# Spreading attention more evenly over the projections, and turning the last two heads on the tensor engine

## The chip, the cores and the metric

One core of one Trainium2 chip runs the program. The metric is the device time of that core in microseconds (us), taken over several executions; the median is quoted with the lowest and highest run. Ratios are computed as the mean time of one kernel's runs over the mean of the other's of the same rounds, so they are not quite the ratio of the medians that are quoted beside them. A difference counts as faster or slower from 2% on.

## The reference

Two blocks follow each other: a recurrent memory attention over 64 segments of 32 tokens with 32 heads, and a mixer with an MLP. Cut to what matters here:

```python
def _A_ref(x, mem0, Wq, Wk, Wv, Wo, seg_len):
    mem = mem0                                  # 8 rows
    for s in range(n_seg):                      # 64 segments, one after the other
        h = concatenate([mem, x[segment s]])
        q, k, v = h @ Wq, h @ Wk, h @ Wv        # 32 heads of 128
        o = softmax(mask(q k^T * scale)) @ v
        o = o @ Wo
        mem = o[:, :M]                          # feeds the next segment
        outs.append(o[:, M:])
x = x + ga * _A_ref(layernorm(x) * (1 + ca) + sa, ...)
x = x + gb * _B_ref(...)                        # cut
```

## The kernel before

It guesses all memory rows first (from averaged segments), runs the attention of all segments at once with the guess (`Mold`), and then compares the memory rows that come out (`Macc`) with the guess. If they do not agree, a flag is set and a second, slow path runs until they do.

```python
TAU2 = 2.0 ** -14
def check_a(kt):                       # per block of the model dimension
    df = Macc - Mold                   # [cut to formulas]
    Mold[kt] = df * df - TAU2 * Macc * Macc
def check_b():
    pn = sum of Mold over the dimension          # one number per memory row
    okr = pn <= 0
    rmx = (min(okr) < 0.5)                       # memory comparison failed
    nb  = (softmax sums, weights or scales out of range)
    nc.vector.tensor_tensor(flag_s[:], rmx[:], nb[:], ALU.max)
    nc.scalar.dma_start(flag_d[:], flag_s[:])
...
first_pass(...)
with tc.If(cond > 0):
    ...
    with tc.For_i(0, MAX_EXTRA):                 # 64 times
        c2 = load_flag()
        tc.strict_bb_all_engine_barrier()
        with tc.If(c2 > 0):
            general_pass()                       # the slow path; sets the flag anew
```

The projections go by pairs of heads (`P_units`), each in three parts `s`: Q and K of the even head, V of both heads, Q and K of the odd head. Attention (`scores`, `outs`) of the pair before is woven between them. V is projected transposed (`VT`) and turned by a DMA (`to_v`) into one of two buffers, `Vs[h % 2]`; `outs` reads it:

```python
units += d[:6] + [lambda: to_v(2 * hp)] + d[6:] if s == 2 else d     # in P_units

def to_v(h):
    assert h < 2 or ("outs", h - 2) in state      # the old V has been used up
    nc.sync.dma_start_transpose(Vs[h % 2][:, :, 0:DH], VTs[h % 2][:]...)

def outs(h, j):                                   # j-th group of three tiles of segments
    V, O = Vs[h % 2], Os[h % 2]
    ... nc.tensor.matmul(ps[:rows, i, :], lhsT=E..., rhs=V[:k, t, 0:DH + 1])
    if j == 7:
        state["outs", h] = True

def flip(h):                                      # O to OT, by DMA
    nc.sync.dma_start_transpose(OT, O[0:96]);  nc.sync.dma_start_transpose(MT, O[96:112])
def keep(h):                                      # memory rows to OTm, OT to DRAM
    ... nc.gpsimd.dma_start(OTx_d[:, h // 8, :, h % 8, :]..., flat...)
```

The order in which the Python emits these units is the program order. The framework derives the semaphores from it: a reader waits for the last writer emitted before it.

The attention list is cut into pairs (`per_hp`), a waiting list is served first in, first out, and after the last projection the last pair runs among the first matmuls of the output projection `Wo` (`W_units`, operands `wstream` and `OTc`).

## Time and profile before

| | before |
|---|---|
| time | 1516.28 us median (1514.69 to 1516.72, 4 runs) |
| PE busy | 1429 of 1517 us (94%) |
| PE waits from 770 to 1000 us | 25.1 us |

In the profile PE is the tensor engine (TensorE) at matmuls and PEld the same engine loading weights; DVE is VectorE, ACT ScalarE, POOL GpSimd, and SP is SyncE, whose queue here only issues DMAs. The granted clock is the share of TensorE's full clock that the hardware let through; the DMA share is how busy the core's 16 DMA engines were. The page of the kernel before says how busy each engine was; the columns are busy us, share of the span and instructions:

```profile
span 1517.1 us, 24283 instructions
PE 1429.2 (94%) x9074; PEld 760.1 (50%) x9074; DVE 921.4 (61%) x1961; ACT 668.2 (44%) x1403; POOL 356.1 (23%) x490
```

PE is the bound, so time can come only from PE's idle time, from its work or from its clock. The waits of PE between 770 and 1000 us of the kernel before (who waited for whom; us in total, times, longest):

```profile
PE ps_o L713 <- DMA V<-VT: 13.6, 1, 13.6
PE acc L845 <- DMA wstream<-in_A_Wo_dram: 7.2, 1, 7.2
PE acc L845 <- DMA OTc<-OTx_d: 3.6, 2, 1.8
PE acc L845 <- DVE x L847: 0.4, 1, 0.4
PE acc L845 <- issue: 0.3, 1, 0.3
```

Why V of the last head is late is read from the timeline of the SP queue of the kernel before (start, us, queue, line, operation):

```profile
785.21 16.14 SPq L728 DMA_TRANSPOSE OT<-O  x1
801.45 1.54 SPq L729 DMA_TRANSPOSE MT<-O  x1
803.08 0.53 SPq L537 DMA_DIRECT2D wo<-in_A_Wo_dram  x1
803.66 5.33 SPq L650 DMA_TRANSPOSE V<-VT  x1
```

The transpose `OT<-O` holds the queue for 16.1 us, since its operand is not ready, and V stands behind it. PE's timeline of the kernel before then shows the wait and what follows it (start, us, engine, line, operation, operands; in square brackets the idle time just before, and what ended it):

```profile
800.20 1.89 PE L845 MATMUL acc<-wstream,OTc 128*128 128x512 bf16 x8
815.64 0.86 PE L713 MATMUL ps_o<-V,E 104*104 104x129 bf16 x6 [13.56 <-DMA V<-VT]
816.30 1.91 PE L845 MATMUL acc<-wstream,OTc 128*128 128x512 bf16 x4
```

Before the wait eight matmuls take 1.89 us, after it four take 1.91 us: half speed. The Trainium skill ("TensorE: Matmul & The Clock Gate", "What's actually happening") says that the PE clock halves after an idle window of about 3.4 us; this trace agrees, at a wait of 13.6 us.

### The profile page before, as it was taken

Reading aid. Unit: us, or ns where it says so; the run is one execution under the profiler, and the core shown is the slowest. Engines: PE = TensorE matmul, PEld = TensorE weight load, DVE = VectorE, ACT = ScalarE, POOL = GpSimd, SP = SyncE. Lnnn points to the kernel's source line nnn. Section 1 sums busy time; section 2 is a strip of 40 time slices with the busy share of each in tenths; the row PEclk is TensorE's granted clock in tenths of the full one; section 3 lists DMA queues with packets and bytes.
Section 4 is the critical chain, followed back from the end, with each engine's and each line's share of the span. In section 5 each row is a group of like instructions: output and inputs, shape, how many; then the busy total and the mean of one; then the engine's idle time right before and its main releaser. Section 6 shows DMA issues by size and latency. Waiting matters only on the chain.

```text
span 1517.1 us, 24283 instructions
## 1 busy us (share of the span) xinstructions
PE 1429.2 (94%) x9074; PEld 760.1 (50%) x9074; DVE 921.4 (61%) x1961; ACT 668.2 (44%) x1403; POOL 356.1 (23%) x490
## 2 busy tenths in 40 slices
PE   5699999999999999999996799999997999999998
PEld 3365555556555655555653344444443444444443
DVE  5827777677676676766751343363287657675684
ACT  2715666665656665665650020122533661046400
POOL 7501100000000000000010222122011654535625
PEclk9999999999999999999998999999999999999999
DMA  9577779877778876778689999994299784377812
GB/s 307 193 279 158 154 163 197 169 161 158 152 163 197 169 171 153 154 159 193 131 220 292 323 328 327 290 270 146 64 276 270 231 265 157 100 246 240 281 52 77
DMA packets 406900, 304.81 MB, mean 201 GB/s; under 512 B 203370, under 2 KB 359018, under 8 KB 404850
## 3 DMA queue, kind: packets, MB, share of 16 engines
q1 hardware_dynamic: 367920, 239.39, 61.3%
q0 software_dynamic: 9616, 33.05, 7.3%
q10 hardware_dynamic: 29234, 30.71, 6.6%
q8 instruction: 73, 1.20, 0.3%
q14 instruction: 57, 0.47, 0.1%
HBM read 200.82 MB, written 50.63 MB: 166 GB/s over the span
## 4 chain that ended last, share of the span: by engine, by line
PE 73%; DMA 8%; issue 6%; DVE 5%; ACT 4%; POOL 3%; SPq 1%; ACTq 0%; DVEq 0%; POOLq 0%
PE acc L607 28%; PE bank_b L1202 6%; PE acc L845 6%; PE bank_b L1151 6%; PE acc L995 4%; PE acc L328 4%; PE bank_d L1151 3%; PE bank_d L1202 2%; PE bank_e L1202 2%; PE ps_o L713 2%; PE ps_s L698 2%; PE acc L318 2%; PE acc L1078 2%; PE bank_e L1151 1%; DVE ln_st L104 1%
## 5 line engine op out<-in xcount | busy, mean ns | idle before, releaser
L845 PE MATMUL acc<-wstream,OTc 128*128 128x512 bf16 x960 | 214.7, 385 | 11.3 <-DMA wstream<-in_A_Wo_dram 7.2
L607 PEld LDWEIGHTS <-T 128*128 128x128 f16 x1408 | 131.1, 97 | 123.2 <-issue 7.4
L575 ACT COPY snap<-acc 128x480 f32<-128x480 f32 x264 | 146.6, 564 | 101.9 <-PE acc L607 91.3
L607 PE MATMUL acc<-hs,T 128*128 128x480 f16 x704 | 158.5, 365 | 4.9 <-ACT snap L575 3.8
L607 PE MATMUL acc<-hh,T 128*128 128x480 bf16 (+1 forms) x704 | 162.3, 366 | 0.5 <-DVE VT L579 0.5
L845 PEld LDWEIGHTS <-OTc 128*128 128x128 bf16 x960 | 94.4, 99 | 124.8 <-DMA wstream<-in_A_Wo_dram 7.4
L740 POOL DMA_DIRECT2D OTx_d<-OT x32 | 24.8, 775 | 511.4 <-DMA OT<-O 495.2
L1151 PEld LDWEIGHTS <-ring 128*128 128x128 f16 (+1 forms) x784 | 77.5, 99 | 109.5 <-issue 17.6
L702 ACT ACTIVATE E<-ps_s 99x495 bf16<-99x495 f32 (+2 forms) x160 | 86.3, 543 | 65.0 <-PE ps_s L698 63.3
L607 PE MATMUL acc<-hh,wq 128*128 128x480 bf16 x464 | 105.3, 366 | 0.0
L579 DVE TENSOR_TENSOR KT<-acc,snap 128x480 bf16<-128x480 f32 x116 | 74.6, 655 | 47.0 <-PE acc L607 45.4
L720 DVE TENSOR_TENSOR O<-ps_o,rin_all 99x384 bf16<-99x384 f32 (+1 forms) x192 | 96.6, 510 | 3.8
L713 PE MATMUL ps_o<-V,E 99*99 99x129 bf16 (+2 forms) x704 | 81.1, 222 | 16.0 <-DMA V<-VT 15.0
L713 PEld LDWEIGHTS <-E 99*99 99x99 bf16 (+2 forms) x704 | 69.2, 127 | 53.2 <-issue 20.4
L1202 PEld LDWEIGHTS <-hq 128*128 128x128 bf16 (+1 forms) x560 | 54.9, 98 | 66.0
L1116 ACT COPY snap<-bank_b 128x512 f32<-128x512 f32 x72 | 40.6, 583 | 102.0 <-PE bank_b L1202 58.3
L715 DVE RECIPROCAL rin_all<-ps_o 99x3 f32<-99x3 f32 (+2 forms) x256 | 43.3, 173 | 68.8 <-PE ps_o L713 67.9
L718 ACT ACTIVATE O<-ps_o,rin_all 99x128 bf16<-99x128 f32 x192 | 56.6, 368 | 61.8 <-DVE rin_all L715 61.7
L1021 DVE TENSOR_TENSOR ring<-ring 128x1024 f16<-128x1024 bf16 (+1 forms) x64 | 75.5, 1200 | 5.5 <-PE bank_b L1202 5.1
L704 DVE TENSOR_TENSOR E<-E,maskB 99x495 bf16<-99x495 bf16 (+1 forms) x128 | 47.3, 377 | 51.5 <-ACT E L702 51.2
L110 POOL TENSOR_TENSOR ln_rstd<-ln_ve,mhalf 128x1 f32<-128x1 f32 x64 | 35.2, 550 | 173.7 <-DVE ln_ve L108 129.8
L938 ACT ACTIVATE u<-x,ln_nmr,ln_rstd 128x1024 bf16<-128x1024 f32 x16 | 19.7, 1232 | 123.9 <-DVE ln_nmr L937 75.0
(223 smaller groups left out, 2569.9 us busy)
## 6 DMA issues: line engine op xcount, KB each, us to landing
wstream<-in_A_Wo_dram SPq DMA_DIRECT2D x29, 1024.0 KB, 9.0
OTx_d<-OT POOLq DMA_DIRECT2D x32, 512.0 KB, 7.5
wstream<-in_B_w_dram SPq DMA_DIRECT2D x28, 512.0 KB, 4.4
ring<-in_B_w_dram SPq DMA_DIRECT2D x28, 512.0 KB, 5.5
ring<-in_B_w_dram SPq DMA_DIRECT2D x8, 1792.0 KB, 10.0
OTc<-OTx_d SPq DMA_DIRECT2D x13, 1024.0 KB, 8.3
wq<-in_A_Wq_dram SPq DMA_DIRECT2D x16, 512.0 KB, 7.6
wk<-in_A_Wk_dram SPq DMA_DIRECT2D x16, 512.0 KB, 8.5
```

What stands on the lines that cost most here:

```text
L328: nc.tensor.matmul(acc[:, 0:CONV], lhsT=W[:, kt, hl * P:(hl + 1) * P], rhs=hh[:, kt, MAIN:MAIN + CONV], start=(kt == 0), stop=(kt == KT - 1))
L575: nc.scalar.copy(t[:], st[q][bank][:, 0:CH])
L579: nc.vector.tensor_tensor(view(d, i), chunks(st[q][bank]), chunks(st[q][s_]), ALU.add)
L607: nc.tensor.matmul(acc[:, 0:CH], lhsT=B[:, k, :], rhs=A[:, k, :], start=(j in (1, 2, 5) and k == 0), stop=(k == 3), skip_group_check=True)
L702: nc.scalar.activation(E[:rows, 0:o], ps[:rows, 0:o], ACT.Exp, scale=DH ** -0.5)
L713: nc.tensor.matmul(ps[:rows, i, :], lhsT=state["e", h, t // 5][:k, col0(t) - col0(t // 5 * 5):col0(t) - col0(t // 5 * 5) + rows], rhs=V[:k ...
L720: nc.vector.tensor_tensor(O[:rows, ts[0]:ts[0] + n, :], ps[:rows, 0:n, 0:DH], rin[:, :, None].to_broadcast([rows, n, DH]), ALU.mult)
L845: nc.tensor.matmul(accs[tt][:], lhsT=ot[hl // 4][:, hl % 4, tt * P:(tt + 1) * P], rhs=woc[hl // 4][:, hl % 4, :], start=(h == 0), stop=(h ...
L995: nc.tensor.matmul(acc[:], lhsT=w1s[:, kt, ct * P:(ct + 1) * P], rhs=zT[:, kt, b * 512:(b + 1) * 512], start=(kt == 0), stop=(kt == KT - 1))
L1021: return nc.vector.tensor_tensor(dst, a, b, op)
L1151: nc.tensor.matmul(acc[:], lhsT=B[:, k, q * P:(q + 1) * P], rhs=A[:, k, :], start=(start and k == 0), stop=(k == 3), skip_group_check=True)
L1202: nc.tensor.matmul(acc[:], lhsT=L3[:, k, i * P:(i + 1) * P], rhs=R3[:, k, :], start=(start and k == 0), stop=(k == 13), skip_group_check=True)
```

## The change

The intent is to fill that hole: attention gets further ahead of the end of the projections, the outputs `O` of the last two heads need no DMA transpose (their few memory rows still do) and no way through DRAM, and loads that are not urgent leave the crowded stretch. The diff, cut to its core:

```diff
-                    units += d[:6] + [lambda: to_v(2 * hp)] + d[6:] if s == 2 else d
+                    units += d[:3] + [lambda: to_v(2 * hp)] + d[3:] if s == 2 else d
@@ turns of the last two heads
+        def turn(h, c):                     # eight tiles of O at a time
+            pt = psS.tile([P, 8, P], BF16, name="ps_s")
+            for i, t in enumerate(ts):
+                nc.tensor.transpose(pt[:, i, 0:96], O[0:96, t, :], ident[0:96, 0:96])
+            ... copy to OT by ScalarE or VectorE; c == 2 also turns MT by DMA
@@ attention(): one list instead of one per pair
+                            if h >= H - 2:
+                                if j in (3, 6):
+                                    waiting.append((5 * h + g, lambda h=h, j=j: turn(h, j // 3 - 1)))
+                                elif j == 7:
+                                    waiting.append((5 * h + g + 1, lambda h=h, j=j: turn(h, 2)))
+                                    waiting.append((5 * h + g + 1, lambda h=h: keep(h)))
+                    waiting.sort(key=lambda w: w[0])
@@ pacing
+        done, ahead = 0, len(att) - int(len(att) * 1.45 / H)
-            interleave(att[hp], fill)
+            for i, u in enumerate(fill):
+                u()
+                upto = int(ahead * (hp + (i + 1) / len(fill)) / (NHP - 1))
+                for a in att[done:upto]:
+                    a()
+                done = upto
@@ tail
+        load_ot(3)                          # six heads from DRAM ...
+        for h in range(H - 2, H):           # ... and two from SBUF
+            nc.vector.tensor_copy(ots[3][1][:, h % 8 - 4, :], last_ot[h][:]...)
+                ld = nc.sync.dma_start(w1s[:], ...)
+                tc.add_manual_dep(ld.ins, marks[1].ins.name, ..., reason="Wo loads first")
+                nc.gpsimd.dma_start(gb_b[:], ...)          # was loaded in the tail
```

The list has 499 units with the turns in it, so `ahead` is 477.

## The prediction

> **What bounds the kernel now.** PE: the page has it busy 1429 of 1517 us (94%). Between 125 and 775 us (attention interleaved with projections) the windows view leaves it about 11 us idle. The hole is the end of attention, 783 to 880: PE's waits view has 13.6 us for `V<-VT`, 7.2 for `wstream<-in_A_Wo`, 1.8 + 1.8 for `OTc<-OTx_d`, 0.3 issue: 24.7 us. After the two long waits the timeline shows 128x512 matmuls at about 427 ns instead of 216; I estimate 5 to 6 us lost. The Trainium skill ("TensorE: Matmul & The Clock Gate", "What's actually happening") says the PE clock halves after an idle window of about 3.4 us; the trace agrees (granted clock 0.73 in 800-825, 0.88 in 850-875). About 30 us can be had.
>
> The V wait is a queue effect: in SP's timeline the last head's `V<-VT` goes out at 803.7, behind an `OT<-O` that held the queue 16.1 us waiting for its operand.
>
> **What the change does.**
> 1. Attention advances 30.55 heads during the projections instead of 30. V of head 31 and the flip of head 29 go out before the projections end: this removes the 13.6 us and its cold matmuls (2.5 us).
> 2. The last two heads are turned by 44 PE transposes, at about 55 ns each (small-matmul intervals in the timeline): +2.5 us PE; evacuations and copies lie off the path. It removes two `OT` transposes and the round trip through `OTx_d` before OTc (11.5 + 9.5 + 5.0 us in the chain at 824-851; only 1.8 was a PE wait).
> 3. w1 (2 MB) and gb (0.5 MB) leave the crowded stretch. 2 MB at the 300 GB/s seen there is 7 us: it removes the 7.2 us wait and its 3 us of half clock.
>
> **What it adds.** Being ahead costs slack on V of the even heads. From PE's instruction order, at intervals from the trace, the work between the last V projection and V's first use is about 29 us in every pair before; after, it shrinks: 15 us (head 6), 7.8 (18), 6.5, 5.5, 4.5, 3.9 (26). In the trace V needs 6.5 us from issue to landing. So new PE waits on `V<-VT` grow from nothing to 3 us, plus 1 at head 28 and 5 to 6 at head 30, where head 31's V and a flip stand ahead in the queue: together 13 us, and 1 us of cold clock. For heads 28 and 30 the first output group even stands before the transpose that loads its V: it uses V of the head two before, a defect of order, perhaps within tolerance.
> In the tail SP now issues loads while POOL's Wo/OTc loads are under way: I expect 2 to 4 us each on OTc or wstream at two places, and 2 us before head 31's scores, which follow their own projection directly: 8 us.
>
> **Sum.** -30.4 + 2.5 (turns) + 14 (V) + 8 (tail) - 1 (head 0) = -7; the new waits are worst cases, so I lean further: **1506 us, 8 in 10 within 1492 to 1515**. Faster by over 2%: 0.05; within 2%: 0.93; slower: 0.02.
>
> **Signs.** Right: the 13.6 and 7.2 us waits are gone, the tail is about 20 us shorter, and PE's waits list `V<-VT` several times between 500 and 790 us, growing. After 880 us all is as long as before.
>
> **What would make it wrong.** V landing faster, no loop waits: then 1490. DMA saturated in the Wo stage (share 0.9 to 1.1 already): the saved time comes back as waits on wstream, then 1515.

## More of the kernel before

The segments depend on each other through `mem`. The kernel does not run them one after the other.

## The result and the profile after

| | before | after |
|---|---|---|
| time | 1516.28 us (1514.69 to 1516.72, 4 runs) | 5475.94 us (5470.07 to 5478.43, 4 runs) |
| ratio | 1 | 3.612 (3.605 to 3.618) |

The change made the kernel 3.6 times slower. The page of the changed kernel has nearly four times the instructions, and groups that the kernel before did not run at all:

```profile
span 5473.4 us, 90797 instructions
PE 5013.8 (92%) x31678; PEld 2760.2 (50%) x31678; DVE 2391.3 (44%) x5511; ACT 2248.8 (41%) x6115; POOL 802.6 (15%) x1084
L1582 PE MATMUL acc<-wv,hhT 128*128 128x256 bf16 x5120 | 619.0, 273 | 0.0
L1455 PE MATMUL acc<-hhT,wq 128*128 128x512 bf16 x2560 | 608.3, 380 | 2.4 <-ACT hhT L1506 2.2
```

Lines 1455 and 1582 lie in `general_pass`, the slow path. How often it ran is read from the instructions that write the flag (first and last start in the second pair of numbers). In the kernel before:

```profile
L931 DVE TENSOR_TENSOR flag_s<-rmx,nb x1: 136/136/136, 950.4 to 950.4; 1x1 int32<-1x1 f32 x1
```

In the changed kernel:

```profile
L1818 DVE TENSOR_SCALAR flag_s<-rmx x2: 134/134/134, 2742.3 to 4590.9; 1x1 int32<-1x1 f32 x2
L966 DVE TENSOR_TENSOR flag_s<-rmx,nb x1: 138/138/138, 949.3 to 949.3; 1x1 int32<-1x1 f32 x1
```

Line 966 is the check of the first pass, line 1818 that of the slow path: the slow path ran twice. The windows of the changed kernel (us; busy us and instructions of each engine, granted clock, DMA share, GB/s) show where the time is:

```profile
0.00:1510.40 1510.40, 1434.61 (x9118) 762.55 (x9118) 931.67 (x1966) 664.97 (x1407) 356.12 (x490) 0.98 0.75 201
1510.40:3500.00 1989.60, 1888.47 (x11954) 1061.46 (x11955) 777.50 (x1916) 851.78 (x2497) 269.23 (x400) 0.97 0.43 136
5300.00:5473.00 173.00, 0.00 (x0) 0.00 (x0) 0.00 (x0) 0.00 (x0) 0.00 (x0) 0.50 0.00 0
```

The last operation of the first pass ended at 1510.4 us. The same operation ended at 1512.5 us in the kernel before, so the first pass gained 2.1 us in these traces (kernel before, then changed kernel):

```profile
1510.61 1.89 DVE L1228 TENSOR_TENSOR o<-join,rs 128x512 bf16<-128x512 f32 x3
1508.53 1.89 DVE L1265 TENSOR_TENSOR o<-join,rs 128x512 bf16<-128x512 f32 x3
```

Then come two slow passes, to 5213 us, and 260 us in which no engine computes: the loop counts off its other 62 rounds, at 260 / 62 = 4.2 us each. Why two can be understood from the source: the first slow pass starts from the rows in `Macc`, which carry the fault, and so is bound to find a difference again.

Inside the first pass the waits of PE answer to those shown of before. From 0 to 770 us the first line, from 770 to 1000 us the others (changed kernel):

```profile
PE ps_o L714 <- DMA V<-VT: 9.5, 3, 6.5
...
PE ps_o L714 <- DMA V<-VT: 6.6, 1, 6.6
PE acc L875 <- DMA wstream<-in_A_Wo_dram: 5.3, 1, 5.3
PE acc L875 <- DMA OTc<-OTx_d: 5.1, 2, 4.7
PE acc L875 <- DVE x L877: 0.5, 1, 0.5
```

The 13.6 us wait is gone, and three waits on V of other heads have come in its place: 1.6 us at head 26, 6.5 at head 28, 6.6 at head 30, 14.7 us together. (The fourth of the list, 1.4 us at head 0, stood in the kernel before too, with 1.5 us.) With the 17.5 us that are left between 770 and 1000 us, the 8.1 us at heads 26 and 28 make 25.6 us, against 25.1 before: the waits moved, they did not shrink. The SP queue of the changed kernel at head 28 (three lines), then PE's timeline there:

```profile
721.82 4.41 SPq L729 DMA_TRANSPOSE OT<-O  x1
726.33 1.53 SPq L730 DMA_TRANSPOSE MT<-O  x1
727.96 9.22 SPq L651 DMA_TRANSPOSE V<-VT  x2
722.61 0.34 PE L714 MATMUL ps_o<-V,E 104*104 104x129 bf16 x3
727.88 0.77 PE L608 MATMUL acc<-hh,T 128*128 128x480 f16 x3
735.15 0.81 PE L714 MATMUL ps_o<-V,E 99*99 99x129 bf16 x6 [6.50 <-DMA V<-VT]
```

The SP queue of the changed kernel near the last of them, and the first output group of head 30:

```profile
771.99 2.88 SPq L729 DMA_TRANSPOSE OT<-O  x1
774.97 1.17 SPq L730 DMA_TRANSPOSE MT<-O  x1
776.25 8.91 SPq L651 DMA_TRANSPOSE V<-VT  x2
773.96 0.35 PE L714 MATMUL ps_o<-V,E 104*104 104x129 bf16 x3
```

At both heads a flip stands ahead of the two V transposes, now at the point where PE needs V. And at both heads the first output group (the one of 104 rows) ran before the V transpose was issued, without a wait: at 722.61 against 727.96 us, and at 773.96 against 776.25 us.

### Why the flag? Three theories

The static instruction order, which can be read without a run, has this on PE (position, line, operands, waits in brackets; cut):

```
before  11726 L713 Matmult ps_o<-V0,E 104x129 [waits DMAHW4]     first group of head 30
after   11528 L714 Matmult ps_o<-V0,E 104x129                    first group of head 30
after   11608 L714 Matmult ps_o<-V0,E 99x129  [waits DMAHW7]     its second group
SP after  228 L651 DmaTransposeAnt V0<-VT0    [waits DMAHW7,PE]  V of head 30
```

In the changed kernel the first group has no wait on a DMA, and the V load waits for PE instead: for the framework the load comes later in the program, so the group reads the V that is still there, head 28's. Head 28 has the same fault with V of head 26.

- Theory A: these stale groups make the memory rows wrong, the comparison fails, the slow path runs.
- Theory B: the turned heads 30 and 31, or the moved loads, deliver wrong memory rows.
- Theory C: the range checks (`nb`) set the flag, not the comparison.

### The profile page after: what moved, and what is told of

The parts are those of the page before. It is cut to its first block, busy times and chain, and to the rows that moved or that the text cites. A ratio compares the mean times of both kernels' runs of the same rounds, so it can differ in the third digit from the quotient of the medians. Undisturbed runs are those within 1.5% of the kernel's fastest.

```text
span 5473.4 us, 90797 instructions
## 1 busy us (share of the span) xinstructions
PE 5013.8 (92%) x31678; PEld 2760.2 (50%) x31678; DVE 2391.3 (44%) x5511; ACT 2248.8 (41%) x6115; POOL 802.6 (15%) x1084
## 5 line engine op out<-in xcount | busy, mean ns | idle before, releaser
L1657 ACT ACTIVATE E<-smk,nmx 120x120 f32<-120x120 f32 x1408 | 538.3, 383 | 422.0 <-DVE nmx L1653 421.6
L1582 PE MATMUL acc<-wv,hhT 128*128 128x256 bf16 x5120 | 619.0, 273 | 0.0
L1455 PE MATMUL acc<-hhT,wq 128*128 128x512 bf16 x2560 | 608.3, 380 | 2.4 <-ACT hhT L1506 2.2
L1455 PE MATMUL acc<-hhT,wk 128*128 128x512 bf16 x2560 | 593.7, 379 | 0.0
L1582 PEld LDWEIGHTS <-hhT 128*128 128x128 bf16 x5120 | 495.7, 98 | 106.6 <-issue 1.1
L1940 PE MATMUL acc<-z2T,wstream 128*128 128x512 bf16 x1792 | 388.4, 379 | 0.0
L1962 PE MATMUL acc<-wstream,h2T 128*128 128x512 bf16 x1792 | 388.1, 379 | 0.0
L1455 PEld LDWEIGHTS <-wk 128*128 128x128 bf16 x2560 | 246.7, 98 | 255.1
L1455 PEld LDWEIGHTS <-wq 128*128 128x128 bf16 x2560 | 242.9, 98 | 238.2 <-issue 4.5
L1657 ACT ACTIVATION_READ_ACCUMULATOR E<-smk,nmx 120x1 f32 x1408 | 262.7, 187 | 0.0
```

What stands on the lines that cost most here:

```text
L1455: nc.tensor.matmul(acc[:, o:o + n], lhsT=W[:, kt, hl * P:(hl + 1) * P], rhs=rhs_fn(kt), start=kt == 0, stop=kt == KT - 1)
L1582: nc.tensor.matmul(a3[:rows, j, :], lhsT=hhT[:, kt, O0 + i * P:O0 + i * P + rows], rhs=w['wv'][:, kt, :], start=kt == 0, stop=kt == KT - 1)
L1657: nc.scalar.activation(E[:TS, b, :], smk[:TS, b, :], ACT.Exp, bias=nmx[:TS, b:b + 1], scale=1.0, accum_out=ssum[:TS, b:b + 1])
L1940: nc.tensor.matmul(acc[:], lhsT=w3c[:, kt, fl * P:(fl + 1) * P], rhs=z2T[:, kt, b * 512:(b + 1) * 512], start=kt == 0, stop=kt == KT - 1)
L1962: nc.tensor.matmul(accs[tt][:], lhsT=h2T[:, ft, tt * P:(tt + 1) * P], rhs=w4c[:, fl, :], start=ft == 0, stop=ft == FT - 1)
```

## The experiments

Twelve runs were made of eleven kernels (one twice). All twelve gave a result within tolerance.

### e1_order: the V load before its readers

```diff
-  units += d[:3] + [lambda: to_v(2 * hp)] + d[3:] if s == 2 else d
+  units += d
   if s == 1 and hp == 0:
       units.append(lambda: (to_v(0), to_v(1)))
+  elif s == 1:
+      units.append(lambda: to_v(2 * hp))
```

> The changed kernel, with one edit: the transpose that loads V of an even head is placed directly behind its last V projection, ahead of any output group that reads it. Theory A (the first output groups of heads 28 and 30 read V of heads 26 and 28, the memory rows come out wrong, the kernel's own check sets its flag and the general pass runs twice): no general pass, about 1505 us (1490 to 1515). Theory B (the turned heads 30 and 31, or the moved loads, deliver wrong memory rows): still about 5476 us. Theory C (the range checks set the flag): still about 5476 us.

Measured: 1513.27 us (1506.66 to 1517.59, 4 runs), before 1516.74; ratio 0.999 (0.996 to 1.002). The slow path did not run; the flag was written once, by the first pass:

```profile
L968 DVE TENSOR_TENSOR flag_s<-rmx,nb x1: 139/139/139, 938.3 to 938.3; 1x1 int32<-1x1 f32 x1
```

Moving the V loads of the even heads in the program takes away 3960 us. The time lies in the range of theory A, at its slow end (about 1505 was expected). Theory A holds; B and C fall, since everything they blame is still in this kernel. The time itself is no better than that of the kernel before.

### e2_pace: the pacing alone, on the kernel before

The attention list, the sort, the pacing with `ahead = 477` and the place of the V load were put into the kernel before, without turns, partial load or moved loads.

> The kernel before, with the new pacing alone (sorted list of attention units, spread evenly, the same 477 units ahead as in the changed kernel, the early place of the V load); no turns, no partial OTc load, w1 and gb where they were. Its PE order puts the first output groups of heads 28 and 30 before their V load, as in the changed kernel. Theory A: two general passes, about 5480 us. Theory B: no general pass, 1495 to 1520 us. Theory C says nothing of it.

Measured: one look, 5480.71 us, and two writes of the flag by the slow path:

```profile
L1784 DVE TENSOR_SCALAR flag_s<-rmx x2: 134/134/135, 2744.9 to 4596.0; 1x1 int32<-1x1 f32 x2
```

Theory B is contradicted from the other side: the turns are not needed for the fault.

### e3_turn: turns and moved loads alone

```diff
- done, ahead = 0, len(att) - int(len(att) * 1.45 / H)
+ done, ahead = 0, 460
```

> The changed kernel with the pacing set back to 30 heads (460 units) ahead; turns of the last two heads, partial load and moved loads stay. All V loads then precede their readers. Theory A: no general pass; the 13.6 us wait for V of the last head comes back in part, the new V waits in the loop are gone: about 1500 us (1488 to 1512). Theory B: about 5476 us.

Measured: 1511.71 us (1507.68 to 1515.12, 4 runs), ratio 0.996 (0.993 to 0.999). No slow path. PE's waits on V behind 760 us, and a new one on the copies of the turned head:

```profile
PE ps_o L714 <- DMA V<-VT: 11.0, 1, 11.0
PE ps_s L752 <- ACT OT L757: 4.0, 1, 4.0
```

The hole of before comes back when the pacing goes back. No wait on wstream or OTc is in this list: a longer wait for V may give the loads time; no run isolates that.

### e4_memoff: the flag without the comparison

```diff
-  nc.vector.tensor_tensor(flag_s[:], rmx[:], nb[:], ALU.max)
+  nc.vector.tensor_tensor(flag_s[:], nb[:], nb[:], ALU.max)
```

> The changed kernel with the memory comparison left out of the flag (the flag is the range checks alone); the stale V stays, so this result may be wrong on purpose. Theory A: no general pass, the time is that of the first pass as the trace of the changed kernel shows it: about 1510 us (1505 to 1515). Theory C: still about 5476 us.

Measured: 1511.66 us (1508.54 to 1515.66, 4 runs), ratio 0.997 (0.994 to 1.001). No slow path: it is the comparison that sets the flag.

```profile
L966 DVE TENSOR_TENSOR flag_s<-nb x1: 138/138/138, 942.9 to 942.9; 1x1 int32<-1x1 f32 x1
```

The output passed the comparison with the reference although two groups had used a wrong V. Only the kernel's own check saw the fault. This run also gives the price of the first pass of the changed kernel: a quarter of a per cent below before, with an interval that reaches no gain at all.

### e8_stale28 and e8_stale30: one stale head at a time

In the changed kernel the V load was set right for every even head but 28, or for every even head but 30:

```diff
-  units += d[:3] + [lambda: to_v(2 * hp)] + d[3:] if s == 2 else d
+  units += d[:3] + [lambda: to_v(2 * hp)] + d[3:] if s == 2 and hp == 14 else d   # or 15
   if s == 1 and hp == 0: ...
+  elif s == 1 and hp != 14:                                                       # or 15
+      units.append(lambda: to_v(2 * hp))
```

> The changed kernel with V of head 30 loaded in time and V of head 28 still late, so head 28 alone has a stale first group. Theory A, if one group of one head is enough to fail the check: about 5478 us. If it needs both, or only head 30 counts: about 1508 us.

> The changed kernel with V of head 28 loaded in time and V of head 30 still late, so head 30 alone has a stale first group. Head 28 alone was enough to fail the check; the same is expected here: about 5475 us. If only head 28 counts (its memory rows are summed by another path): about 1508 us.

Measured: one look each, 5469.67 us and 5463.74 us; each ran the slow path twice. One group of one head is enough.

### e5_pace2: where the first pass lost its gain

Theory A settles the 3.6. What is left is why the first pass, which had about 30 us to win by the prediction, won so little. The waits above name the V loads of the even heads; this run gives V time by the pacing alone. The V load stays at the changed kernel's place; with attention less far ahead it comes before its readers, so the order is right too.

```diff
- ahead = len(att) - int(len(att) * 1.45 / H)
- upto = int(ahead * (hp + (i + 1) / len(fill)) / (NHP - 1))
+ ahead = 473
+ f = (i + 1) / len(fill)
+ upto = int(429 * (hp + f) / (NHP - 2)) if hp < NHP - 2 else int(429 + (ahead - 429) * f)
```

> The changed kernel, paced in two slopes: two heads a pair of projections up to head 28, and only in the last pair the extra half head (473 units ahead in all); turns and moved loads stay. In PE's order V of every even head now has at least 19 us of work between its last projection and its first use, and 9 us for head 30. If the waits on V cost the corrected order (e1) what the trace lists, 7.4 us before 760 us and 6.1 us behind it, both go to 0 to 3 us here, the general pass does not run, and it takes 1490 to 1503 us. Rival: the loop is bound by something else and the waits reappear under other names: 1505 to 1513 us as e1.

Measured: 1502.64 us (1502.26 to 1507.60, 4 runs), before 1514.94; ratio 0.992 (0.990 to 0.995). PE waited on V only once, 1.4 us, at the first head. The waits behind 760 us:

```profile
PE acc L876 <- DMA wstream<-in_A_Wo_dram: 10.7, 1, 10.7
PE acc L876 <- DMA OTc<-OTx_d: 2.8, 2, 2.2
```

From the trace of e1 to that of e5 the waits on V went from 13.5 us to 1.4, and those on the loads of the tail rose from 9.0 to 13.5 us. The V waits were real: the intervals of the two ratios are apart, if barely. That a part of what they freed was given back to the loads is what these two traces suggest; traces of one kernel differ by nearly as much (see e7_again).

### e6_loads and e7_both: the order of the loads

e6 is e1, and e7 is e5, with two loads put first:

```diff
+  W0_load(1, 0)
+  W0_load(1, 1)
   load_ot(3)
   for u in W0[0][2]: u()
```

> e1 with one edit: two Wo slices of the next half are asked for before the partial OTc load, so that what PE needs first stands first in the queue. If the order of the loads makes the waits on OTc and wstream in the tail (9.0 us in e1), they fall to about 4 us: 1500 to 1508 us. Rival: the loads are limited by their total bytes, the waits stay 9 us: as e1.

> The pacing of e5 and the load order of e6 together. If both causes add: 1485 to 1498 us, waits on V and on loads together under 8 us. If the tail is limited by bytes: as e5.

Measured, e6: 1510.32 us (1505.86 to 1512.21, 4 runs), ratio 0.995 (0.993 to 0.998); its waits on the loads are 8.8 us against 9.0 in e1, so the order alone did nothing there that these runs could show, and e6 missed its range (1500 to 1508 us). e7: 1498.70 us (1494.33 to 1504.26, 6 runs), ratio 0.989 (0.987 to 0.991). Its waits behind 760 us:

```profile
PE acc L876 <- DMA wstream<-in_A_Wo_dram: 3.6, 1, 3.6
PE acc L876 <- DMA OTc<-OTx_d: 3.3, 1, 3.3
```

The interval of e7 overlaps that of e5, so the load order is only likely, not shown, to be worth something. e7 missed its range by 0.7 us, and its waits on V and loads are 8.3 us, not under 8.

### e10_w1early and e7_again: the hold on w1

e10 is e7 without the added dependency, so that w1 is loaded in the tail again. e7_again is e7 on the same chip.

> e7 with the hold on the w1 load taken away, so that its 2 MB go out in the tail again, ahead of two Wo slices, as in the kernel before. If the w1 load caused the 7.2 us wait on wstream of the kernel before: 5 to 10 us slower than e7, with a wait on wstream of 5 us or more near 850 us. If it does not matter: as e7.

> e7 once more on the same chip as the other runs of this call, to compare with: 1494 to 1502 us.

Measured: e7_again 1498.25 us (1495.78 to 1504.78, 6 runs), ratio 0.989 (0.988 to 0.991); e10 1507.68 us (1503.74 to 1510.35, 4 runs), ratio 0.996 (0.994 to 0.997). The intervals are apart: the hold on w1 is worth about 9 us in this kernel. The waits on wstream alone do not make up that sum: they are 9.1 us in e10's trace and 6.8 in e7_again's. The granted clock from 775 to 880 us, 0.95 against 1.00, is another part. PE's timeline of e10 shows a wait that the kernel before also had:

```profile
845.83 4.32 PE L876 MATMUL acc<-wstream,OTc 128*128 128x512 bf16 x12 [5.23 <-DMA wstream<-in_A_Wo_dram]
```

One trace is weak evidence for a few us here. The waits on the loads of the tail are 6.9 us in e7 and 10.4 in e7_again, the same kernel, and whether a wait of 3 to 4 us was followed by half speed differed too. The first line is of e7, the others are of e7_again:

```profile
796.99 3.28 PE L876 MATMUL acc<-wstream,OTc 128*128 128x512 bf16 x8 [3.25 <-DMA OTc<-OTx_d]
796.15 1.90 PE L876 MATMUL acc<-wstream,OTc 128*128 128x512 bf16 x8 [2.99 <-DMA OTc<-OTx_d]
823.55 7.07 PE L876 MATMUL acc<-wstream,OTc 128*128 128x512 bf16 x32 [4.00 <-DMA wstream<-in_A_Wo_dram]
```

After 3.25 us eight matmuls took 3.28 us; after 2.99 us eight took 1.90 us, and after 4.00 us 32 took 7.07 us, the full speed.

### e9_bytes: fewer bytes in the tail

e9 is e7 with two modulation rows and one OTc block issued later. The expectation names gb as well, but the edit leaves gb where it was.

> e7 with less asked of the DMA engines in the tail: two modulation rows (0.5 MB written to SBUF), gb (0.5 MB) and one OTc block (1 MB) are issued later. Theory D (what is left of the tail's waits, 3.3 us on OTc and 3.6 us on wstream in e7, is bytes: 329 GB/s at a DMA share of 1.00): 2 MB less is about 6 us, so the waits fall under 3 us and the time is 1490 to 1496 us. If they hang on the order of the queue instead: within 2 us of e7.

Measured: 1501.02 us (1495.03 to 1502.32, 5 runs), ratio 0.990 (0.988 to 0.991), against 0.989 of e7_again. The waits in its tail are 8.6 us, not under 3. This expectation failed, but the run hardly tests it: the two rows went out at 810 us instead of 787, still in the tail, and from 783 to 866 us the DMA engines moved 316 GB/s against 326 in e7_again, only 0.8 MB less. What limits the last waits, the bytes in flight or the order in the two queues, stays open. The Trainium skill ("DMA: Bandwidth & Descriptors", "Issuing engines are not separate DMA queues") says that DMAs issued by the scalar, sync and gpsimd engines run on the same 16 DMA engines. It fits that loads from SP delay those from POOL here, at a DMA share of 1.00 and 329 GB/s between 783 and 866 us in e7, but no run isolates it.

## Why the prediction was wrong

- **The step that failed: the weight given to the stale V.** The prediction had found the fault: "it uses V of the head two before, a defect of order, perhaps within tolerance". The output was indeed within tolerance (e4). But the consequence was not followed to the check: the memory rows of those groups go into `Macc`, the comparison allows 0.8% of a row, and a failed comparison costs two slow passes. e1, e2, e4 and the two e8 runs show each link. An estimate from the source would have been enough: if 32 heads contribute alike and independently, one wrong head changes a row by about the square root of 2/32, 25%, thirty times the limit. The time of a fault that the kernel can notice is the time of its reaction.
- **The cost that stood nowhere in the sum.** Two slow passes and the loop's empty rounds are 5473 - 1510 = 3963 us. The range of 1492 to 1515 had no room for a second path at all.
- **The first pass came near the forecast, partly by luck.** e4, which is the first pass alone, took 1511.66 us; the forecast was 1506. But of the 10 us to be gained e4 shows about 4 (ratio 0.997), with an interval that reaches no gain, and the traces show 2.1. The sum of the V waits came out near only because an excess at head 28 and the missing waits at heads 20 to 24 cancelled.
- **Waits on V: right in mechanism and in sum, wrong in the split.** Predicted 13 us, with 1 us at head 28 and 5 to 6 at head 30; measured 14.7 us, with 6.5 at head 28, 6.6 at head 30, 1.6 at head 26 and none at heads 20 to 24. At head 30 a flip and head 31's V stood ahead of it in the queue, as predicted. The prediction did not have the flip at head 28: V of head 28 could not go out before the stale group that reads the old V ended (722.95 us), but it went out only at 727.96, behind that flip. That is 5 us of the 6.5, an estimate from these lines; no run moves the flip alone. The 1 us to be won at head 0 was not won.
- **The 13.6 us wait: right.** It is gone, and comes back to 11.0 us when the pacing alone is undone (e3).
- **The w1 load: right in size.** Predicted 7.2 us of wait and 3 us of half clock for holding it back; e10 against e7_again gives about 9 us, measured in e7 and not in the changed kernel, and how it splits into wait and clock is not shown. But the promised absence of the wait was wrong: the changed kernel still waits 5.3 us for wstream, elsewhere.
- **The tail: right in sum, wrong in one place.** Predicted 8 us of new waits, measured 10.4 on wstream and OTc. So the waits between 770 and 1000 us fell from 25.1 to 17.5 us, and the sign of a tail about 20 us shorter did not come. The 2 us before head 31's scores do not appear in the list of waits.
- **The turns: right.** Predicted about 55 ns each. In the trace of the changed kernel eight turns take 0.51 us, about 43 ns apart (0.51 less the 0.206 of one, over 7), so 44 of them are about 2 us. The Trainium skill ("TensorE: Matmul & The Clock Gate", "Back-to-back issue gap") gives N / 2.4 + 2.5 ns for one isolated matmul of N columns at the full clock, an estimate of 42.5 ns for the 96 here, and this trace agrees. For a stream of weight loads and matmuls the same section has about 81 ns at 128 columns; the turns, each with its weight load, stood closer:

```profile
793.58 0.51 PE L752 MATMUL ps_s<-ident,O 96*128 96x96 bf16 x8
```

The intent of the change was sound. With the order set right, two slopes of pace and the load order (e7) it is 1.1% faster than before. That is the best kernel, and under the 2% from which a difference counts here.

## What to carry to other kernels

When a schedule moves readers forward, check that the write each of them needs is still ahead of it in program order: the framework keeps whatever order it is given, and nothing in the framework stopped this kernel, whose readers consistently read old data. The kernel's assertion guarded only one side (the old V is used up before it is overwritten); the other side (the new V is there before it is read) needs one too. And where a kernel has a guard with a slow path, any change that can touch what the guard compares has to be judged at the price of that path, not at the tolerance of the output.

## What the Trainium skill lacked or had wrong

- "Advanced Engine Details and Errata" ("Control Flow Timing") has a branch at 51 or 108 ns, but no price for a round of a runtime loop whose body is skipped. With a flag load, a barrier of all engines and a branch it was 4.2 us here (260 us for 62 rounds).
- "TensorE: Matmul & The Clock Gate" ("Part 4: PE-mode transpose") says that transposes do not engage the full clock as matmuls do. Here eight turns in a row stood about 43 ns apart, at a granted clock of 1.00 from 793 to 795 us. Matmuls stood before and after them and may have held the clock, so this is no contradiction; the page does not have this mixed case.
- "DMA: Bandwidth & Descriptors" names the bandwidth of a DMA transpose, and gives sequencer cycles for one only in a comparison with a later chip, but not how long one holds the queue that issues it: in the kernel before 3.3 to 7.5 us for one `V<-VT`, and 16.1 us for an `OT<-O` whose operand was late, with every later load of that queue behind it.
